# Folding the first batch's short chunk ahead of its products, in a Fourier-mixing and gated feed-forward kernel

## The chip, the cores and the metric

The kernel runs on one core of one Trainium2 chip. The metric is the device time of one execution in microseconds (us). Engine names are those of the profile: PE is TensorE's matmul, PEld its weight load, DVE is VectorE, ACT ScalarE, POOL GpSimd, SP SyncE, which here issues DMAs.

## The reference

```python
def reference(x, moe_w_gate, moe_w_val, moe_w_out):   # x: 8 x 3008 x 256
    X = np.fft.fft(x, axis=1)
    X = np.fft.fft(X, axis=2)
    a = X.real.astype(np.float32).reshape(8 * 3008, 256)
    g = a @ moe_w_gate                                  # 256 x 1536
    silu = g * (1.0 / (1.0 + np.exp(-g)))
    val = a @ moe_w_val
    return (silu * val @ moe_w_out).astype(np.float32)  # 1536 x 256
```

So there is a real part of a two-dimensional Fourier transform of each batch (over 3,008 rows and 256 columns), and then a gated feed-forward layer on each of the 24,064 rows. Inputs and output are float32.

## The kernel before

**The mathematics.** The kernel does not transform the columns (called d) of x. It folds that transform into the weights: `Wp` and `Wq` are the gate and value weights multiplied by a cosine table `CD` and a sine table `SDt` (`half_w` for the first 512 columns of the weights, `weight_op` inside the main loop for the other two blocks of 512). `Wm` is `Wq` with rows scaled by the column `m2`, for the mirrored rows of the output. What is left of the transform over rows is done by products with tables of cosines and sines (`Tab`), on data that has been folded by symmetry: row n with row M - n, and quarters with each other. The results are `Pt` (even part) and `Qt` (odd part), tiles of up to 512 transformed rows, which are the moving operand of the feed-forward products.

**Chunks.** The rows of a batch's quarter are cut into a long chunk of 128 (A) and a short one of 60 (C). For the first batch, `place` puts rows in order by a product with a 0/1 matrix (`putA`, `putC`) into PSUM; `sums` adds (k = 0) or subtracts (k = 1) the falling rows from SBUF into `SA` (chunk A) and `SC` (chunk C), on DVE; `fold_d` folds SA over d on POOL into `EOA`, which ACT copies as bfloat16 to `EOb`, and `half_folded` multiplies that by the tables. For chunk C, `direct` writes unfolded halves `SBc` on DVE straight from PSUM, and `unfolded` multiplies both halves, 16 products in all. `row0` adds the products of the column d = 0. `transform` copies one half of the result by ACT (`od`) and adds or subtracts it on DVE to write `Pt` and `Qt`. In this start-up the order on each engine is the order written in the code.

**The part for the odd rows.** The second part of the first batch (job (0, 1)) needs `BBa` for chunk A and `BBc` for chunk C, which lies in `St`. Before the change POOL makes them in the main loop's time out of EOA and SC: `quarter_rows` twice, and for each of two q a sum, a difference and five scalings by the row signs `sgn` and `sgo`.

**The main loop.** Its units (t, f) are 24 tiles t of up to 512 rows and 12 blocks f of 128 hidden columns. Each unit has gate and value products in PSUM (`g` and `v`, three buffers each), Silu on ACT, products on DVE or POOL into `hp` and `hm`; `OWork` multiplies these by `Wo` (`o`, two buffers), ACT evicts and SP stores. Which engine does what is read from `KINDS`, one digit a unit: bit 1 has the odd row added ahead by ACT ("seed", L1425), bit 2 has the gate split (two gate products of PE instead of three, with work on DVE), the higher bits give products to POOL; "w" (tile 0 and two units of tile 1) is a unit with all six products.

**The planner.** The main loop is not written in order. `S.add` collects operations with an engine, a duration that the author assumed, what they read, write and need; `S.run` then plays a list schedule over the engines and emits the instructions in that order. `SHIFT` and `BIAS` (per tile and kind of operation) move due times; `S.run` is told from when each engine is free. DMA arrivals are stand-ins with an assumed latency. The chip runs each engine's instructions in that order, each waiting for its inputs.

**Queues.** Loads of x for the first batch go out on SP and on ACT's queue, weight loads on POOL's queue, in `load_w`: W0 (first 512 columns of the gate and value weights), then the rest into the space of `XA` (`Wraw`), in blocks of 512 columns. Loads of chunk C of batches 0 and 1 (L156 and L158) follow on SP behind two copies of zeros (L564) that wait for a memset of `zeros`. At most eight DMAs of SP are under way, since each waits for the eighth before it. `Wo` (L1978) is issued on POOL behind the BBc work.

The rows that the steps touch: L378 weight loads, L426 `place`, L435 `sums`, L492 and L493 `fold_d`, L480 `half_folded`, L487 `unfolded`, L529 `direct`, L460 to L464 `half_w`, L607 `row0`, L638 and L643 `transform`, L352 and L356 angles, L359 and L362 sines and cosines, L694 row signs, L1818 to L1833 weight blocks in the loop, L1352 gate and value products, L1387 to L1411 whole units, L1614 products with Wo.

Of the kernel before, what the change touches and what calls it, by code (L numbers as in the profile page):

```python
# [12 lines left out]
F32 = mybir.dt.float32  # L13
# [18 lines left out]
def kernel(  # L32
# [8 lines left out]
    nc = tc.nc  # L41
# [71 lines left out]
    sgn = const.tile([P, 1], F32, name="sgn")  # L113
    XA = const.tile([P, 8, 2, D], F32, name="XA")
# [6 lines left out]
    Wraw = [XAw[:, i * 4 * T:(i + 1) * 4 * T].rearrange("p (n f) -> p n f", n=2) for i in range(2)]  # L121

# [110 lines left out]
    SBc = tp.tile([P, 2, 2, 2, 2, P], BF16, name="SBc")  # L233
# [13 lines left out]
    nc.vector.memset(sel, 0.0)  # L247
    xf = XC0.rearrange("p a q d -> p (a q d)")
# [18 lines left out]
    fall_c(1, 0, nc.scalar)  # L267
    fall_c(1, 1, nc.scalar)
# [18 lines left out]
    def more_iotas():  # L287
        nc.gpsimd.memset(putC, -1.0)
        for hi in range(2):
            pm = 64 * hi + NCR  # L290
            nc.gpsimd.iota(putC[:, pm - NCR:pm], pattern=[[-2 * LC, NC_], [2, LC]], base=2 * (NCR - LC) + hi, **iota)
        pts(putC, putC, scalar1=pcol, scalar2=1.0, op0=Alu.is_equal, op1=Alu.mult)
# [41 lines left out]
    nc.vector.memset(EOf[:, 1, :, P:P + 1], 0.0)  # L334
    vts(m2, pcol, scalar1=0.0, scalar2=-2.0, op0=Alu.not_equal, op1=Alu.mult)
    vts(sgn, half, scalar1=1.0 / 32, scalar2=1.0, op0=Alu.mult, op1=Alu.add)
    sgo = const.tile([P, 1], F32, name="sgo")
    vts(sgo, pc, scalar1=float(NCR), scalar2=-2.0, op0=Alu.is_equal, op1=Alu.mult)
    vts(sgo, sgo, scalar1=1.0, scalar2=sgn, op0=Alu.add, op1=Alu.mult)
    vts(wC, pc, scalar1=float(LC - 1), scalar2=-0.5, op0=Alu.is_equal, op1=Alu.mult)  # L340
    vts(wC, wC, scalar1=1.0, scalar2=None, op0=Alu.add)
# [31 lines left out]
    def load_w(fc, only=(0, 1)):  # L373
        for i, src in ((0, moe_w_gate), (1, moe_w_val)):
            if i not in only:
                continue
            dst = W0[i] if fc == 0 else Wraw[i][:, :, (fc - 1) * T:fc * T]
            nc.gpsimd.dma_start(out=dst, in_=src.rearrange("(no p) f -> p no f", p=P)[:, :, fc * T:(fc + 1) * T])  # L378
# [7 lines left out]
    turns(ti[0], kf, 0)  # L386
    turns(ti[1], kf, 1)
    nc.gpsimd.dma_start(out=XC0[NCR:64 + NCR + 1:64, 2:4, 0],
                        in_=rows_at(0, 0, [[2 * R * D, 2], [R * D, 2], [1, D]]))
    more_iotas()  # L390
# [3 lines left out]
    tp.tile([P, 1900], F32, name="pad")  # L394

    def ce_angles(ch):
        rr, ra = ce_angle[ch]
        angles(rr, kf, ch, ti[ch])
        magnitude(ra, rr)

    def ce_tables(ch):
        rr, ra = ce_angle[ch]
        sine(ch, 0, NCE, rr)
        cosine(ch, 0, NCE, ra)

    ce_angles(0)
    nc.vector.memset(Tab[:, :, :, :, NOO - 1:NOO], 0.0)
    ce_tables(0)
    ce_angles(1)
    ce_tables(1)  # L410
# [8 lines left out]


# [15 lines left out]

    def halves(SB, S, k, a=0):

        nc.scalar.copy(SB[:, k, 0, a:a + 2], S[:, k, a:a + 2, :, P:0:-1])
        nc.scalar.activation(SB[:, k, 1, a:a + 2], S[:, k, a:a + 2, :, P:D], AF.Copy, scale=(-1.0 if k else 1.0))  # L440
# [81 lines left out]
    def direct(k):  # L522
        for a in range(2):
            down = XC0[:, 2 + a, ::-1, :]
            for hf, r_ in ((0, slice(P, 0, -1)), (1, slice(P, D))):
                x_, y_ = psC[a][:, :, r_], down[:, :, r_]
                if k and hf:
                    x_, y_ = y_, x_
                vtt(SBc[:, k, hf, a], x_, y_, op=(Alu.add, Alu.subtract)[k])  # L529
# [24 lines left out]
    direct(0)  # L554
    direct(1)
    sums(SC, 0, XC0, psC)
    start_acc(1)
    X3c = XC.rearrange("p a q d -> p (a q d)")
    zeros = Af.rearrange("p a b d -> p (a b d)")[:, 0:D]
    hd = tp.tile([P, 2, 2, 1], F32, name="hd")  # L560
    ptt(hd, SA[:, 0, 0:2, :, 0:1], SA[:, 0, 2:4, :, 0:1], op=Alu.add)
    nc.gpsimd.memset(zeros, 0.0)
# [6 lines left out]
    nc.vector.memset(SDt[:, :, 0:1], 1.0)  # L569
# [93 lines left out]
    unfolded(0, SBc)  # L663
    transform(0, 0, (0,), acc)
    for a in (0, 2):
        half_folded(1, a)
    nc.gpsimd.iota(kfO, pattern=[[4, G]], base=1, **iota)
    load_w(2)
    turns(rrO[:, 0].bitcast(I32), kfO, 0)
    turns(rrO[:, 1].bitcast(I32), kfO, 1)  # L670
    for k in range(2):
        half_w(0, k, psO, "o")
    unfolded(1, SBc)
    for q in range(2):
        row0(0, q, acc[1][q])
    sums(SC, 1, XC0, psC)
# [6 lines left out]
    for q in range(2):  # L683
        quarter_rows(ptt, EOA[:, 0, :, q, :], EOA[:, 1, :, q, :], BBa[:, q])

    for q in range(2):
        S, Dd = SC[:, 0, :, q, :], SC[:, 1, :, q, :]
        E, O = EOf[:, 0, 0:2], EOf[:, 1, 0:2]
        ptt(E[:, :, 0:P], S[:, :, P:0:-1], S[:, :, P:D], op=Alu.add)
        ptt(O[:, :, 0:P], Dd[:, :, P:0:-1], Dd[:, :, P:D], op=Alu.subtract)  # L690
        for dst, src, sg in ((BBc[:, q, 0, 0], E[:, 0, 0:P], 1.0), (BBc[:, q, 0, 1], E[:, 1, 0:P], -1.0),
                             (BBc[:, q, 1], O[:, :, 0:P], None), (BBc[:, q, 1, 0, 0:1], S[:, 1, 0:1], -1.0),
                             (BBc[:, q, 1, 1, 0:1], S[:, 0, 0:1], 1.0)):
            pts(dst, src, scalar1=sgn if sg else sgo, scalar2=sg or 1.0, op0=Alu.mult, op1=Alu.mult)  # L694


# [37 lines left out]
    def rows(r0, n, step):  # L734
# [4 lines left out]
    WP_ACT = ()  # L739
    C1_AT = 10  # L740
    A1_AT = 21
    C2_AT = 38
    A1_LOAD = 8
# [26 lines left out]
        (16, 'SP'): 3.25,  # L770
        (14, 'EV'): -1.0,
        (16, 'HP'): -2.25,
        (16, 'EG'): -1.6,
        (19, 'SM'): 2.5,
        (8, 'EG'): 1.05,
        (23, 'VM'): 3.15,
        (9, 'HP'): -2.2,
        (17, 'EV'): 0.2,
        (14, 'VG'): 4,
        (3, 'SM'): -1.5,  # L780
        (18, 'HP'): -2.5,
# [17 lines left out]
        (1, 'EG'): -1.1,  # L799
        (2, 'ES'): 2.05,  # L800
        (2, 'EV'): -1.35,
        (3, 'PUT'): -4.6,
        (3, 'SP'): 3.35,
        (3, 'VM'): -0.3,
        (4, 'ROW'): -5,
        (3, 'ROW'): 1.6,
        (3, 'HP'): -0.65,
        (3, 'EG'): -0.35,
        (0, 'HM'): 2.2,
        (0, 'EG'): -2.2,  # L810
        (0, 'HP'): -1.5,
        (0, 'VAL'): -1.2,
        (0, 'SEED'): 2.0,
        (0, 'SM'): 0.9,
        (0, 'VG'): -0.75,
        (0, 'HG'): -1.25,
        (0, 'SP'): 3.6,
        (0, 'ROW'): -0.3,
        (0, 'OD'): 4.5,
        (0, 'EV'): 0.4,  # L820
        (0, 'VM'): -0.25,
        (0, 'ES'): -1.7,
        (0, 'PUT'): 0.1,
        (1, 'EV'): 4.45,
        (1, 'ES'): 3.05,
        (2, 'SP'): -1.4,
        (1, 'SEED'): 0.9,
        (1, 'HM'): 1.95,
        (2, 'SEED'): -0.4,
        (1, 'SM'): 0.2,  # L830
        (1, 'SP'): 0.9,
        (2, 'VG'): -0.9,
        (1, 'ROW'): 1.3,
        (1, 'OD'): -1.15,
        (1, 'FOLD'): -0.15,
        (1, 'HG'): 1.6,
        (1, 'VG'): 0.15,
        (1, 'PUT'): -1.25,
        (1, 'VAL'): 0.25,
        (2, 'PUT'): 0.65,  # L840
        (2, 'VAL'): -0.25,
        (2, 'OD'): 0.75,
        (2, 'HP'): -0.75,
        (2, 'VM'): -0.5,
        (2, 'FOLD'): 0.5,
        (2, 'HG'): 0.75,
        (2, 'EG'): -0.25,
        (3, 'SEED'): 1.4,
        (3, 'OD'): 0.4,
        (3, 'HG'): -1.45,  # L850
        (3, 'GM'): -1.65,
        (3, 'EV'): 1.4,
        (3, 'VAL'): -2.2,
        (3, 'HM'): 0.55,
        (3, 'ES'): -0.85,
        (3, 'VG'): 0.1,
        (3, 'FOLD'): -0.5,
        (5, 'HM'): 2.2,
        (5, 'ROW'): -1.85,
        (4, 'VG'): 0.85,  # L860
        (4, 'HP'): 5,
        (4, 'SEED'): -2.7,
        (4, 'EG'): 3.7,
        (4, 'PUT'): -0.1,
        (4, 'SP'): -0.65,
        (4, 'OD'): 1.6,
        (4, 'VM'): 2.2,
        (4, 'HG'): -0.8,
        (4, 'HM'): 1.25,
        (4, 'SM'): -0.45,  # L870
        (4, 'VAL'): -0.5,
        (4, 'ES'): -0.35,
# [1162 lines left out]
```

## Time and profile before

| what | us |
|---|---|
| median of 3 runs (604.97 to 605.37) | 605.32 |
| the profiled execution | 605.64 |
| its span | 603.9 |
| busy PE / DVE / ACT / POOL | 595.8 / 575.9 / 564.2 / 510.2 |
| first gate product of tile 0 (L1352) starts | 21.19 |
| first product with Wo (L1614) starts | 48.52 |

The granted TensorE clock is 1.00 in every stretch of this profile. Busy time of PE is modelled from starts and lengths, so it covers small gaps. Times in the text are from the start of the span; "from ... to" of a group in the timeline runs from the first start to the last end.

### The profile page before, as it was taken

To read this page: it belongs to the slowest core of one execution; us is meant where nothing else is said; L and a number is where in the kernel's file an instruction comes from. 1 tells how busy PE (TensorE), PEld (TensorE's weight loads), DVE (VectorE), ACT (ScalarE), POOL (GpSimd) and SP (SyncE) were. 2 spreads that over 40 slices of the span, in tenths; PEclk is the share of its full clock that TensorE was granted. 3 is DMA by queue.
4 is the path that set the end of the run, shared out by engine and by line. 5 is a ranking of instruction groups with operands and counts; after the bars stand their busy time and mean duration, and the time that the engine had idled before them with its cause. 6 is when DMAs were issued, how large, how long until landed. Compare 5 with 4: busy or idle time off the path is not lost.

```text
span 603.9 us, 12610 instructions
## 1 busy us (share of the span) xinstructions
PE 595.8 (99%) x4058; PEld 392.6 (65%) x4058; DVE 575.9 (95%) x1069; ACT 564.2 (93%) x1086; POOL 510.2 (84%) x469
## 2 busy tenths in 40 slices
PE   8999999999999999999999999999999999999997
PEld 6546666666666666666666666666666666666686
DVE  9999999999999999999999999999999999999993
ACT  7798999999999999989999999999999999999994
POOL 8937999999798999996999988797997467687772
PEclk9999999999999999999999999999999999999999
DMA  8886446244715413454254112036111212111112
GB/s 228 112 148 160 112 121 176 63 129 112 198 42 123 126 60 121 120 134 115 64 115 123 53 47 81 17 102 187 50 60 38 63 46 63 37 54 51 54 53 80
DMA packets 51054, 57.91 MB, mean 96 GB/s; under 512 B 7254, under 2 KB 38170, under 8 KB 50988
## 3 DMA queue, kind: packets, MB, share of 16 engines
q1 hardware_dynamic: 47334, 53.97, 32.7%
q0 software_dynamic: 3216, 2.36, 3.2%
q10 hardware_dynamic: 438, 0.77, 0.5%
q8 instruction: 32, 0.52, 0.4%
q14 instruction: 34, 0.28, 0.2%
HBM read 29.43 MB, written 24.65 MB: 90 GB/s over the span
## 4 chain that ended last, share of the span: by engine, by line
PE 86%; ACT 3%; POOL 3%; DMA 2%; issue 1%; DVE 1%; SPq 0%; ACTq 0%; POOLq 0%
PE o L1614 38%; PE g L1352 25%; PE v L1352 18%; PE g L1770 2%; PE o L1770 2%; DMA XA<-in_x_dram 1%; POOL hm L1563 1%; PE v L1614 1%; POOL SDf L174 1%; ACT sg L1408 0%; ACT sg L1387 0%; DMA out_dram<-ev 0%; PE o L601 0%; PE g L601 0%; PE o L1818 0%
## 5 line engine op out<-in xcount | busy, mean ns | idle before, releaser
L1563 POOL TENSOR_TENSOR hm<-sv 128x1024 bf16<-128x1024 f32 (+2 forms) x137 | 254.6, 1862 | 55.5 <-ACT sv L1539 21.2
L1555 DVE SCALAR_TENSOR_TENSOR sv<-es,v 128x512 f32<-128x512 f32 (+2 forms) x266 | 176.8, 671 | 6.2 <-PE v L1352 3.3
L1566 DVE TENSOR_TENSOR hp<-sp,v 128x512 bf16<-128x512 f32 (+2 forms) x241 | 160.6, 672 | 4.6 <-PE v L1352 2.3
L1614 PE MATMUL o<-Wo,hm 128*128 128x256 bf16 (+1 forms) x1128 | 162.5, 273 | 0.0
L1614 PE MATMUL o<-Wo,hp 128*128 128x256 bf16 (+1 forms) x1104 | 159.8, 272 | 0.0
L1614 PEld LDWEIGHTS <-hm 128*128 128x128 bf16 (+2 forms) x1140 | 111.8, 98 | 56.5 <-issue 1.7
L1614 PEld LDWEIGHTS <-hp 128*128 128x128 bf16 (+2 forms) x1140 | 111.9, 98 | 55.4 <-issue 1.5
L1539 ACT ACTIVATE sv<-g 128x512 f32<-128x512 f32 (+2 forms) x181 | 117.9, 673 | 4.3 <-PE g L1352 2.2
L1464 ACT ACTIVATE sp<-g 128x512 f32<-128x512 f32 (+2 forms) x181 | 111.6, 625 | 3.1 <-PE g L1352 2.1
L1425 ACT ACTIVATE v<-bc,w 128x512 f32<-128x512 bf16 (+2 forms) x151 | 107.9, 718 | 3.0 <-DVE hm L1411 1.2
L1352 PE MATMUL g<-Pt,Wp 128*128 128x512 bf16 (+2 forms) x288 | 107.9, 375 | 0.2 <-DVE Qt L643 0.2
L1352 PE MATMUL v<-Pt,Wp 128*128 128x512 bf16 (+2 forms) x288 | 105.2, 374 | 0.7 <-ACT v L1425 0.6
L1352 PE MATMUL g<-Qt,Wq 128*128 128x512 bf16 (+2 forms) x288 | 105.1, 375 | 0.0
L1487 ACT ACTIVATE es<-v 128x512 f32<-128x512 f32 (+2 forms) x151 | 93.3, 620 | 2.5 <-DVE sv L1555 1.1
L1489 DVE SCALAR_TENSOR_TENSOR es<-bc,w,v 128x512 f32<-128x512 bf16 (+2 forms) x123 | 90.1, 735 | 2.6 <-PE v L1352 1.1
L1352 PEld LDWEIGHTS <-Wp 128*128 128x128 bf16 x576 | 56.2, 98 | 27.4 <-issue 1.6
L1352 PE MATMUL g<-Qt,Wm 128*128 128x512 bf16 (+2 forms) x195 | 72.9, 376 | 0.5 <-ACT sg L1387 0.3
L1468 DVE SCALAR_TENSOR_TENSOR sg<-bc,w,g 128x512 f32<-128x512 bf16 (+2 forms) x93 | 67.2, 724 | 1.6 <-PE g L1352 1.3
L1539 ACT ACTIVATE sv<-sg 128x512 f32<-128x512 f32 (+2 forms) x93 | 64.5, 698 | 0.9 <-DVE sg L1532 0.9
L1532 DVE SCALAR_TENSOR_TENSOR sg<-sg,g 128x512 f32<-128x512 f32 (+2 forms) x93 | 61.6, 662 | 0.9 <-PE g L1352 0.4
L1352 PE MATMUL v<-Qt,Wm 128*128 128x512 bf16 (+2 forms) x165 | 61.6, 374 | 0.4 <-ACT es L1487 0.4
L1536 ACT ACTIVATE sp<-g 128x512 f32<-128x512 f32 (+2 forms) x93 | 56.9, 612 | 4.6 <-DVE sg L1532 4.4
(199 smaller groups left out, 754.3 us busy)
## 6 DMA issues: line engine op xcount, KB each, us to landing
out_dram<-ev SPq DMA_DIRECT2D x96, 128.0 KB
XA<-in_x_dram SPq DMA_DIRECT2D x30, 256.0 KB
XA<-in_x_dram SPq DMA_DIRECT2D x112, 64.0 KB
XC<-in_x_dram SPq DMA_DIRECT2D x30, 120.0 KB
XC<-in_x_dram SPq DMA_DIRECT2D x105, 32.0 KB
bc<-br SPq DMA_DIRECT2D x19, 128.0 KB
St<-Fc SPq DMA_DIRECT2D x12, 128.5 KB
out_dram<-ev SPq DMA_DIRECT2D x12, 120.0 KB
```

The costliest lines, as they stand in the source:

```text
L1352: nc.tensor.matmul(ps[:, :n], Wt[:, gv, fs], src[:, :n], start=start, stop=stop, skip_group_check=True)
L1425: nc.scalar.activation(T_[kv][:, :w], bc[t][:, :w], AF.Copy, scale=w0[:, 1, f:f + 1])
L1464: nc.scalar.activation(sp_to()[:, :w], T_[kg][:, :w], AF.Silu)
L1468: nc.vector.scalar_tensor_tensor(T_[keg][:, :w], bc[t][:, :w], w0[:, 0, f:f + 1], T_[kg][:, :w], op0=Alu.mult, op1=Alu.add)
L1487: nc.scalar.activation(T_[kes][:, :w], T_[kv][:, :w], AF.Copy, scale=2.0 if on_pool(u) > 1 else 1.0)
L1489: nc.vector.scalar_tensor_tensor(T_[kes][:, :w], bc[t][:, :w], w0[:, 1, f:f + 1], T_[kv][:, :w], op0=Alu.mult, op1=Alu.add)
L1532: nc.vector.scalar_tensor_tensor(T_[kgm][:, :w], T_[keg][:, :w], 2.0, T_[kg][:, :w], op0=Alu.mult, op1=Alu.subtract)
L1539: nc.scalar.activation(sv()[:, f % 2, w - 1::-1, 1], T_[kgm if by_dve else kg][:, :w], AF.Silu)
L1555: nc.vector.scalar_tensor_tensor(sv()[:, f % 2, w - 1::-1, 0], T_[kes][:, :w], 2.0, T_[kv][:, :w], op0=Alu.mult, op1=Alu.subtract)
L1563: nc.gpsimd.tensor_tensor(hts_(t)[1][:, f - 1:f + 1, :w], sv()[:, :, :w, 1], sv()[:, :, :w, 0], op=Alu.mult)
L1566: nc.vector.tensor_tensor(hts_(t)[0][:, f, :wp], T_[ksp][:, :wp], T_[kv][:, :wp], op=Alu.mult)
L1614: nc.tensor.matmul(st["ps"][:n, j, :], hts[t][minus][:, f, c:c + n], Wo[:, f, :], start=(f == 0), stop=(f == nF - 1))
```

## The change

It has four parts.

1. Chunk C of the first batch is folded over d by DVE (`fold_c`, from SC into a bfloat16 tile `EB` that lies in EOf) before its products: `folded_c` issues 8 products where `unfolded` issued 16. `direct` and `SBc` go. ACT later scales EB by row signs into BBc (`signed_op`, at unit 8); two one-column products on DVE write BBc's column 0. POOL's loop over q goes, and its two `quarter_rows` become three operations over both q.
2. The sums of chunk A are ordered by pairs of quarters (sum and difference of a pair together), both accumulators are begun early, `half_folded(1, 0)` stands before `place(XC0)`, and 8 + 4 warm products on PE stand where there were 28.
3. The rest of the weights comes in two DMAs of 1,024 columns instead of four of 512. Two x loads move from ACT's queue to SP's. The memsets of `zeros` and `Z0` move from POOL to the opening of DVE, the row signs and weights from DVE to POOL, the d tables ahead of the sines on ACT.
4. The planner's inputs change: `WM_ACT` is empty (all four Wm blocks on POOL), `WP_ACT` gives one Wp block to ACT, `KINDS` of tiles 1 to 16, `BIAS` of tiles 0 to 17, unit numbers of folds, the assumed arrival of weights and the times from which engines are free. From tile 18 on KINDS and BIAS are the same.

```diff
+    nc.vector.memset(Z0, 0.0)
+    zeros = Af.rearrange("p a b d -> p (a b d)")[:, 0:D]
...
-    fall_c(1, 0, nc.scalar)
-    fall_c(1, 1, nc.scalar)
+    fall_c(1, 0, q)
+    fall_c(1, 1, q)
...
+    vts(rrd, prod, scalar1=D - 1, scalar2=None, op0=Alu.bitwise_and)
+    def row_weights():
+        pts(wC, pc, scalar1=float(LC - 1), scalar2=-0.5, op0=Alu.is_equal, op1=Alu.mult)
+        pts(wC, wC, scalar1=1.0, scalar2=1.0, op0=Alu.mult, op1=Alu.add)
+        pts(putC, putC, scalar1=pcol, scalar2=1.0, op0=Alu.is_equal, op1=Alu.mult)
+    def row_signs():
+        pts(m2, pcol, scalar1=0.0, scalar2=-2.0, op0=Alu.is_gt, op1=Alu.mult)
+        pts(sgn, half, scalar1=1.0 / 32, scalar2=1.0, op0=Alu.mult, op1=Alu.add)
+        pts(nsgn, sgn, scalar1=-1.0, scalar2=1.0, op0=Alu.mult, op1=Alu.mult)
...
-    def load_w(fc, only=(0, 1)):
+    def load_w(first, only=(0, 1)):
...
-            dst = W0[i] if fc == 0 else Wraw[i][:, :, (fc - 1) * T:fc * T]
-            nc.gpsimd.dma_start(out=dst, in_=src.rearrange("(no p) f -> p no f", p=P)[:, :, fc * T:(fc + 1) * T])
+            if first:
+                nc.gpsimd.dma_start(out=W0[i], in_=w_[:, :, 0:T])
+            else:
+                nc.gpsimd.dma_start(out=Wraw[i][:, :, 0:Dff - T], in_=w_[:, :, T:Dff])
...
+    d_tables()
+    sine(0, 0, NCE, ce_angle[0][0])
...
-    def unfolded(eo, SB):
+    def folded_c(eo):
         for a in range(2):
             for q in range(2):
                 dst, rhs = set_cols(acc[eo][q], Tab[:, 1, q, eo], a)
-                for hf in range(2):
-                    nc.tensor.matmul(dst, SB[:, eo, hf, a, q, :], rhs, start=False, stop=(a == 1 and hf == 1),
-                                     skip_group_check=True)
+                nc.tensor.matmul(dst, EB[:, eo, a, q, :], rhs, start=False, stop=a == 1, skip_group_check=True)
+    def fold_c(eo):
+        s_ = SC[:, eo]
+        vtt(EB[:, eo], s_[:, :, :, P:0:-1], s_[:, :, :, P:D], op=(Alu.add, Alu.subtract)[eo])
...
     psA = place(XA, putA, 4, ((psG, "g"), (psV, "v")))
-    warm(28)
-    sums(SA, 0, XA, psA, (0, 1))
-    vts(rrd, prod, scalar1=D - 1, scalar2=None, op0=Alu.bitwise_and)
-    sums(SA, 0, XA, psA, (2, 3))
-    opposite(0)
+    warm(8)
+    for a0 in (0, 2):
+        sums(SA, 0, XA, psA, (a0, a0 + 1))
+        sums(SA, 1, XA, psA, (a0, a0 + 1))
+    start_acc(0)
+    start_acc(1)
     fold_d(0, 0)
+    load_w(1, (0,))
     weigh_ce()
-    load_w(0, (0,))
+    half_folded(0, 0)
+    warm(4)
+    fold_d(1, 0)
+    load_w(1, (1,))
+    half_folded(1, 0)
+    psC = place(XC0, putC, 2, ((psG, "g"), (psV, "v")))
+    opposite(1)
     fold_d(0, 2)
-    load_w(0, (1,))
-    opposite(1)
-    d_tables()
-    sums(SA, 1, XA, psA)
-    start_acc(0)
-    half_folded(0, 0)
-    if 0:
-        warm(0)
-    psC = place(XC0, putC, 2, ((psG, "g"), (psV, "v")))
+    fold_d(1, 2)
+    load_w(0)
     half_folded(0, 2)
-    for a in (0, 2):
-        fold_d(1, a)
-    load_w(1)
-    direct(0)
-    direct(1)
-    sums(SC, 0, XC0, psC)
-    start_acc(1)
+    half_folded(1, 2)
+    for k, a in ((0, 0), (1, 0), (0, 1)):
+        sums(SC, k, XC0, psC, (a,))
+    fold_c(0)
+    nc.vector.memset(SDt[:, :, 0:1], 1.0)
+    sums(SC, 1, XC0, psC, (1,))
+    fold_c(1)
+    for k in range(2):
+        vts(BBc[:, :, 1, k, 0:1], SC[:, 0, 1 - k, :, 0:1], scalar1=(nsgn, sgn)[k], scalar2=None, op0=Alu.mult)
...
-    WP_ACT = ()
+    WP_ACT = ((1, 1),)
...
-    WM_ACT = ((1, 0), (1, 1))
+    WM_ACT = ()
+    SIGN_AT = 8
...
+    def signed_op():
+        for k, sg in enumerate((sgn, nsgn)):
+            S.add("ACT", 0.3, lambda k=k, sg=sg: nc.scalar.activation(BBc[:, :, 0, k], EB[:, 0, k], AF.Copy, scale=sg),
+                  r=[(("fold",), "E")], w=[(("st", 0), k)])
+        S.add("ACT", 0.5, lambda: nc.scalar.activation(
+            BBc[:, :, 1, :, 1:P], EB[:, 1, :, :, 1:P].rearrange("p a q d -> p q a d"), AF.Copy, scale=sgo),
+              r=[(("fold",), "E")], w=[(("st", 0), 0)])
...
-    for fc, at in ((1, 0.0), (2, 4.0)):
+    for fc in (1, 2):
         for gv in range(2):
-            S.add("DMA", 0.01, lambda: None, w=[(("W",), (fc, gv))], lat=at + gv)
+            S.add("DMA", 0.01, lambda: None, w=[(("W",), (fc, gv))], lat=1.5 * gv)
...
-    S.run({'DVE': 1.2, 'ACT': 0.7, 'POOL': 13.0, 'PE': 0.0})
+    S.run({'DVE': 1.2, 'ACT': 0.9, 'POOL': 3.0, 'PE': 0.0})
```

In the changed program the products of weight blocks stand at L1804 (L1818 before) and the loop's gate and value products at L1338 (L1352 before).

More of the change, by code (lines that the diff above doesn't have):

```diff
@@ L662 @@
     first_tile = {(b, part): tile_of(b * H + part * 2 * G) for b, part in jobs}
-    unfolded(0, SBc)
+    folded_c(0)
     transform(0, 0, (0,), acc)
[L665 to L670, printed above, removed]
     for k in range(2):
         half_w(0, k, psO, "o")
-    unfolded(1, SBc)
+    folded_c(1)
     for q in range(2):
         row0(0, q, acc[1][q])
-    sums(SC, 1, XC0, psC)
     transform(0, 0, (1,), acc)
@@ L682 @@
         nc.scalar.activation(Wm[:, :, fs], Wq[:, :, fs], AF.Copy, scale=m2)
[L683 to L694, printed above, removed]
+    nc.gpsimd.iota(kfO, pattern=[[4, G]], base=1, **iota)
+    turns(rrO[:, 0].bitcast(I32), kfO, 0)
+    turns(rrO[:, 1].bitcast(I32), kfO, 1)
+    E_, O_ = EOA[:, 0].rearrange("p a q d -> p q a d"), EOA[:, 1].rearrange("p a q d -> p q a d")
+    ptt(BBa[:, :, 0], E_[:, :, 0:4:3, 0:P], E_[:, :, 2:0:-1, 0:P], op=Alu.subtract)
+    ptt(BBa[:, :, 1], O_[:, :, 0:2, 0:P], O_[:, :, 2:4, 0:P], op=Alu.subtract)
+    ptt(BBa[:, :, 1, :, 0:1], E_[:, :, 3::-3, P:P + 1], E_[:, :, 1:3, P:P + 1], op=Alu.subtract)
     tmp_ctx.close()
@@ L817 @@
[L817 to L836, printed above, removed]
@@ new lines @@
+        (6, 'PUT'): -2.6,
+        (6, 'ROW'): -1.1,
+        (6, 'VG'): 0.9,
+        (6, 'HM'): 0.6,
+        (6, 'OD'): -1.5,
+        (7, 'HP'): 0.25,
+        (6, 'ES'): -0.5,
+        (7, 'ROW'): -0.95,
+        (7, 'GM'): -2.25,
+        (7, 'HM'): 0.15,
+        (7, 'SM'): 0.5,
+        (7, 'OD'): -1,
+        (7, 'HG'): 0.25,
+        (7, 'VG'): 1,
+        (7, 'VM'): -0.5,
+        (7, 'SP'): 0.25,
+        (8, 'ES'): 1.4,
+        (8, 'SM'): -0.85,
+        (8, 'OD'): -0.3,
+        (8, 'VAL'): 1.85,
@@ L1699, in fn @@
                 if kind == "A":
-                    queue[what] = fold_steps(nc.gpsimd, XA, *coef_a(b), q, slice(0, P))
+                    queue[what, q] = fold_steps(nc.gpsimd, XA, *coef_a(b), q, slice(0, P))
                 else:
@@ L1907 @@
               17: [lambda: S.add("POOL", 0.8, halve_tables, w=[(("Tab",), "z")])],
-              6: [lambda: S.add("POOL", 0.5, clear_d0, w=[(("Z0",), k) for k in range(2)])]}
+              6: []}
+    before.setdefault(SIGN_AT, []).append(signed_op)
     def row_width(t):
```

596 lines of the change are left out of this document (288 added, 308 removed).

## The prediction

> **What bounds the kernel now.** I read the busy totals first, then busy time by stretch, then the start-up in the timeline, then the DMA issues. The busy totals:
>
> ```profile
> PE 595.8 (99%) x4058; PEld 392.6 (65%) x4058; DVE 575.9 (95%) x1069; ACT 564.2 (93%) x1086; POOL 510.2 (84%) x469
> ```
>
> PE is the bound, but its busy time is modelled, so I count its work instead. From the first gate product (21.19 us) on, the kernel issues 3,910 matmuls: 1,198 of 512 columns, 2,280 of 256, 130 of 480, 278 between 188 and 377 and 24 of one column. In the chain of waits eight of 256 columns take 0.87 us (0.109 each) and four of 512 take 0.86 (0.215 each), so a matmul costs 0.417 ns a column plus 2.5 ns (25 ns each for the one-column ones). That is 571.1 us of dense work. The last matmul ends at 599.8, so PE stood still for about 7.5 us after 21.19. By start-to-start gaps 2.7 us of that lie before 48.5, 4.3 us between 48.5 and 430, the rest later, where the order of the changed program is nearly or wholly the old one. Busy time by stretch (columns: stretch, length, PE, PEld, DVE, ACT, POOL, clock, DMA share, GB/s):
>
> ```profile
> 21.19:48.50 27.31, 26.04 (x146) 12.17 (x144) 25.98 (x51) 25.90 (x48) 14.79 (x26) 1.00 0.78 125
> 48.50:200.00 151.50, 150.31 (x1024) 100.14 (x1023) 145.44 (x258) 142.84 (x275) 145.35 (x137) 1.00 0.47 128
> ```
>
> In the first stretch DVE and ACT are as full as PE: there the eviction engines pace PE. So three things count: when the first gate product starts, how much DVE and ACT hold PE up in tile 0, and the gaps of the middle. The start-up, in order of time:
>
> ```profile
> 9.59 1.09 POOL L492 TENSOR_TENSOR EOA<-SA 128x512 f32<-128x512 f32 x1 [1.21 <-DVE SA L435]
> 10.62 0.82 POOL L378 DMA_DIRECT2D W<-in_moe_w_gate_dram  x1
> 12.04 1.10 PE L426 MATMUL g<-XC,putC 128*128 128x512 f32 x2
> 12.59 0.62 ACT L493 CAST EOb<-EOA 128x512 bf16<-128x512 f32 x1 [0.44 <-POOL EOA L492]
> 13.55 0.76 DVE L529 TENSOR_TENSOR SBc<-g,XC 128x256 bf16<-128x256 f32 x2
> 16.20 0.68 DVE L435 TENSOR_TENSOR SC<-g,XC 128x512 f32<-128x512 f32 x1
> 20.59 1.27 DVE L643 TENSOR_TENSOR Qt<-g,od 128x188 bf16<-128x188 f32 x6
> 17.28 1.48 SPq L564 DMA_DIRECT2D XC<-Af  x2
> 18.80 12.20 SPq L156 DMA_DIRECT2D XC<-in_x_dram  x15
> ```
>
> DVE works without a break from 8.29 to 22.4; the last columns of Qt and the second Wp copy release tile 0. The DMA issues (KB, us to landing):
>
> ```profile
> XA<-in_moe_w_gate_dram POOLq DMA_DIRECT2D x2, 256.0 KB, 6.6
> XA<-in_moe_w_val_dram POOLq DMA_DIRECT2D x2, 256.0 KB, 8.2
> W<-in_moe_w_gate_dram POOLq DMA_DIRECT2D x1, 256.0 KB, 4.6
> W<-in_moe_w_val_dram POOLq DMA_DIRECT2D x1, 256.0 KB, 5.0
> ```
>
> **The change, part by part.** *Opening, to the first sum.* DVE loses seven one-column operations (3.88 to 4.62, 0.7 us) and gains the Z0 memset (64 words took it 0.11, 256 took POOL 0.33, so 0.3 to 0.7 for 384; I take 0.35), the zeros (0.3) and rrd (0.25, moved from between the sums). The ScalarE queue loses two DMA issues (3.20 to 5.54), so prodd comes near 3.1 instead of 5.6 and the d tables (four rows, 1.5 us) go ahead of the sines at no cost: ACT stood idle there. Their issues go to SP, which stood idle from 3.33 to 6.0 and has room for the 2.3 us; past that, rise_c would come later by the rest. The sums begin near 8.4 instead of 8.29. POOL gains seven one-column operations (0.20 to 0.27 each, L694 and L444) ahead of its first fold, which moves from 9.59 to about 9.8; who reads them (weigh_ce, place C, the two one-column products) comes 1.5 us later or more.
>
> *Sums, folds, place C.* The eight SA sums follow each 0.60 apart as before and end near 13.3. But place(XC0) now stands on PE behind half_folded(1, 0), which waits for a second POOL fold behind a weight DMA: 9.8, fold 1.09, issue 0.82, fold 1.10, cast 0.62, four products at 0.16, with 0.05 a hand-over, gives 14.1. Its first pair takes 1.1 (12.04 to 13.14), so SC can start near 15.3, and DVE stands idle for 2 us. That is the price of the new order.
>
> *From SC to the first gate product.* Gone: eight direct operations (13.55 to 16.28, 2.7 us) and sixteen products of 377 columns; new: two folds of 512 columns, two one-column operations, eight products. No row shows a DVE fold with both inputs in SBUF: the 512-column sums take 0.68, POOL's fold 1.10, the 377-column rr operation 0.60 to 0.85; I take 0.7 of the range 0.6 to 1.1, as the sums are nearest. Three SC sums 15.3 to 17.15, first fold to 17.85, products 0.64 and the od copy 0.47 to 19.0; meanwhile fourth sum, second fold and two small ones keep DVE until 19.3. Six Pt puts 1.2, Wp copy 0.68: 21.2. The second od is there at 21.1 (eight half_w products 0.87, four products 0.64, row0 0.65, copy 0.47), so Qt runs 21.2 to 22.4. The second pair of half_w needs the PSUM tile that the Wp copy frees at 21.2; eight products later, at 22.1, the first gate product starts, against 21.19: **+0.9** (0.4 to 1.6).
>
> *PE's work in the main loop.* The listing has one 512-column product more (one gate split fewer): **+0.2**. The 16 warm products and eight others that go lie in waiting time: nothing. Half the weight issues (two of 0.73) go on POOL; that is cover for its own turns, not path.
>
> *Tile 0.* DVE loses one Wp copy (0.68). ACT loses two Wm copies (0.70 each), gains a Wp copy (0.59) and three sign operations (0.5 each by the 512-column copies, halved for 256; 1.1 together). POOL loses the BBc work (25.9 to 33.2, 7.3 us); two Wm more (0.69 each) fit there. The Wo load, issued at 33.19 and 11.8 us on its way, goes out near 25, and the listing puts the first Wo product after 18.4 us of matmuls instead of 24.1: PE has work that needs neither DVE nor ACT. ACT's queue from its first sg (24.0) to its first od is 18 sg at 0.455, four Wq at 0.50, four sines at 0.83 and 2.0 for the rest, 15.5 us, for 15.5 us of matmuls that began 1.9 us sooner and may run some 0.7 ahead; later ACT catches up. So PE loses some 1.3 us before it reaches the place of 48.5, where it lost 2.7: **-1.4** (-2.2 to 0).
>
> *The middle.* The listing has five seeds fewer (ACT 0.72 + 0.62 each off, 0.735 each onto DVE) and three products more on POOL with their copies (0.6 on ACT): ACT -4.9 us, DVE about -1. With the gaps at 4.3 us and their releasers DVE and ACT, I take **-0.9**; the new order could as well cost 2 or save 2.5.
>
> Sum: 0.9 + 0.2 - 1.4 - 0.9 = -1.2. The profiled execution took 605.64 (span 603.9 and 1.7 around it), 0.3 above the median, so 604.4 there and 604.1 against the median. About 0.2% (1.2 us) is what a measurement of this kernel tells from no change; the forecast sits at that edge.
>
> **Rivals.** *Late weights (slower).* The zeros now come from DVE near 8.4, so SP's two L564 issues and the XC loads, held until 17.28 and 18.80 by POOL's memset, follow near 9.8 and share the DMA engines with W0 and the weight rest. W0 landed in 4.6 to 5.0 us without them, the rest in 6.6 to 8.2 beside them. PE needs the whole val rest after 4.1 us of products, at 26.4; issued at 16.6 it lands at 24.8 if 8.2 holds. But four pieces took from 15.3 to about 28.8 (19.1 + 9.7, the longest landing); if the rest takes that long again, it lands near 29, PE waits 2.9 and some 0.6 comes out of later gaps: 606.5 to 607. It decides from a landing past 26.4. The Trainium skill, DMA: Bandwidth & Descriptors, "Why a DMA increments its semaphore by 16 and not by 1", says that a copy uses the largest number of DMA engines up to 16 that divides both slowest dimensions, so a four-partition XC load would burden four engines and a weight load would wait for those; by it this rival holds. The trace, which names no engine, agrees in that the last weight landed at 9.7 us beside such loads.
>
> *A colder clock (slower).* 28 warm products become 12, and by my chain PE idles 1.2 us before each half_folded. The granted clock is 1.00 in every stretch, but the first 52 products took 4.62 us where the 28 took 1.73. If PE ran at half rate from 11 on, the products on the path (first pair of folds 0.6, place C 1.1, folded_c and half_w 1.2 each time) would double and cost some 2.9: 607.0. The Trainium skill, TensorE: Matmul & The Clock Gate, "What's actually happening", gives an idle window of about 3.4 us before half rate; by that no gap here is long enough.
>
> *The order does not fit (slower).* The planner sees the weights at 0 and 1.5 us and POOL free at 3.0; if the middle gains 2 us of gaps instead of losing 0.9: 607.0.
>
> *More gain.* Middle gaps shrink by 2.2 and tile 0 by 1.6: 602.7. Nothing goes lower, as the dense work stays. That fewer DMAs mean fewer bytes isn't so: 1,024 KB either way.
>
> **Chances.** Forecast 0.48 (own range 603.1 to 605.5; 0.31 faster, 0.17 same); late weights 0.22 (0.18 slower, 0.04 same); clock 0.06 slower; order 0.10 (0.08 slower, 0.02 same); more gain 0.14 faster. Faster 0.45, same 0.23, slower 0.32. The range 602.7 to 607.0 leaves out the ends of the rivals.
>
> **What would show it.** Right: DVE idle about 2 us ahead of SC near 15.3; first gate product near 22.1; no PE wait for a DMA at L1804; fewer than 1.5 us of gaps in tile 0; Wo landed before 40. Wrong: SC before 14.5, a first gate product before 21.2 or past 23, a weight product released by a DMA, a clock under 1.00, or middle gaps above 5 us.

## The result, and the profile after

The changed kernel is slower: 610.72 us (median of 4 runs, 610.21 to 612.68) against 605.35 for the kernel before (4 runs, 604.97 to 605.67), a ratio of 1.0095 with a 95% interval of 1.0072 to 1.0118. Its profiled execution took 610.45, with a span of 608.6. The forecast was 604.1, with a range of 602.7 to 607.0.

First the page's busy totals and its row of the granted clock (40 equal slices, in tenths of full speed):

```profile
PE 592.9 (97%) x3978; PEld 391.9 (64%) x4035; DVE 573.7 (94%) x1058; ACT 559.9 (92%) x1081; POOL 510.3 (84%) x462
...
PEclk9899999999999999999999999999999999999999
```

No engine has more work than before (POOL 0.1 us), and yet the span is 4.7 us longer. The second slice (15 to 30 us) has a clock of 8 where the others have 9. So the loss is in the start-up, and its timeline comes next (start, length, engine, line, operation; in brackets the idle time ahead of it and what ended it):

```profile
10.01 1.48 SPq L565 DMA_DIRECT2D XC<-Af  x2
11.54 16.68 SPq L160 DMA_DIRECT2D XC<-in_x_dram  x15
...
13.10 0.74 POOL L388 DMA_DIRECT2D W<-in_moe_w_val_dram  x1
...
15.73 1.29 DVE L447 TENSOR_TENSOR SC<-g,XC 128x512 f32<-128x512 f32 x2 [2.32 <-PE g L438]
18.91 0.69 DVE L447 TENSOR_TENSOR SC<-v,XC 128x512 f32<-128x512 f32 x1 [1.89 <-issue]
...
20.39 0.34 PE L493 MATMUL v<-Tab,EOf 128*128 128x377 bf16 x1 [2.70 <-DVE SDt L556]
...
22.96 0.58 PE L467 MATMUL o<-W,CD 128*128 128x256 bf16 x2 [1.54 <-DMA W<-in_moe_w_val_dram]
...
28.24 0.38 PE L1338 MATMUL g<-Pt,Wp 128*128 128x480 bf16 x1 [0.50 <-DVE Qt L643]
```

SP sends the two copies of zeros at 10.01 and the fifteen chunk C loads of batch 1 from 11.54 on, 7.3 us sooner than before. The third sum of SC waits 1.89 us; the label says "issue", but the wait was on the count of the last XC0 load and ended 0.04 us after that load's last piece landed (18.83). Then PE waits for the value half of W0 (L467), and the first gate product starts at 28.24 instead of 21.19. The clock by stretch, with the same columns as before, and the DMA issues:

```profile
22.00:24.00 2.00, 1.04 (x6) 0.71 (x6) 1.84 (x9) 0.00 (x0) 2.00 (x5) 0.74 0.95 186
24.00:26.00 2.00, 2.00 (x9) 0.92 (x8) 0.27 (x1) 0.58 (x1) 2.00 (x2) 0.50 0.43 93
```

```profile
XA<-in_moe_w_gate_dram POOLq DMA_DIRECT2D x1, 512.0 KB, 10.2
XA<-in_moe_w_val_dram POOLq DMA_DIRECT2D x1, 512.0 KB, 13.2
W<-in_moe_w_gate_dram POOLq DMA_DIRECT2D x1, 256.0 KB, 9.2
W<-in_moe_w_val_dram POOLq DMA_DIRECT2D x1, 256.0 KB, 9.8
```

The two halves of W0 took 9.2 and 9.8 us to land, where they took 4.6 and 5.0: that is the fault in two rows. From 22.95 to 26.36 PE ran at half rate. From the first gate product to the end of the last matmul it took 576.8 us, 1.8 less than before (578.6). So 7.05 us were lost ahead of it and 1.8 won behind it.

### The profile page after: what moved, and what is told of

Same layout as the page of the kernel before. It is cut to its first block, busy times and chain, and to the rows that moved or that the text cites. A ratio compares the mean times of both kernels' runs of the same rounds, so it can differ in the third digit from the quotient of the medians.

```text
span 608.6 us, 12502 instructions
## 1 busy us (share of the span) xinstructions
PE 592.9 (97%) x3978; PEld 391.9 (64%) x4035; DVE 573.7 (94%) x1058; ACT 559.9 (92%) x1081; POOL 510.3 (84%) x462
## 4 chain that ended last, share of the span: by engine, by line
PE 83%; DVE 4%; issue 2%; POOL 2%; ACT 2%; DMA 1%; SPq 0%; DVEq 0%; ACTq 0%
PE o L1600 36%; PE g L1338 23%; PE v L1338 18%; PE g L1756 2%; PE o L1756 2%; DVE sv L1541 1%; DVE hp L1552 1%; POOL hm L1549 1%; DVE es L1475 1%; PE v L1600 1%; DMA XC<-in_x_dram 0%; POOL SDf L178 0%; DVE sg L1518 0%; ACT sp L1450 0%; PE g L601 0%
## 5 line engine op out<-in xcount | busy, mean ns | idle before, releaser
L1552 DVE TENSOR_TENSOR hp<-sp,v 128x512 bf16<-128x512 f32 (+2 forms) x238 | 157.7, 670 | 5.2 <-PE v L1338 4.0
L1525 ACT ACTIVATE sv<-g 128x512 f32<-128x512 f32 (+2 forms) x182 | 120.9, 679 | 3.8 <-PE g L1338 3.3
L1411 ACT ACTIVATE v<-bc,w 128x512 f32<-128x512 bf16 (+2 forms) x146 | 105.4, 723 | 2.1 <-DVE sv L1541 1.0
L1338 PE MATMUL g<-Pt,Wp 128*128 128x512 bf16 (+2 forms) x280 | 104.7, 375 | 1.5 <-ACT sp L1522 0.7
L1338 PE MATMUL v<-Pt,Wp 128*128 128x512 bf16 (+2 forms) x287 | 105.6, 375 | 0.4
L1475 DVE SCALAR_TENSOR_TENSOR es<-bc,w,v 128x512 f32<-128x512 bf16 (+2 forms) x128 | 93.1, 732 | 3.2 <-PE g L1338 0.5
L1473 ACT ACTIVATE es<-v 128x512 f32<-128x512 f32 (+2 forms) x146 | 90.4, 621 | 4.6 <-PE v L1338 2.5
L1338 PE MATMUL g<-Qt,Wq 128*128 128x512 bf16 (+2 forms) x250 | 91.9, 374 | 0.4
L1338 PEld LDWEIGHTS <-Wp 128*128 128x128 bf16 x576 | 56.1, 97 | 26.3 <-DVE Qt L643 0.8
L1338 PE MATMUL g<-Qt,Wm 128*128 128x512 bf16 (+2 forms) x192 | 71.9, 376 | 0.5
L1338 PEld LDWEIGHTS <-Wq 128*128 128x128 bf16 x430 | 41.9, 98 | 27.6 <-issue 3.5
```

The source lines that it names most:

```text
L1338: nc.tensor.matmul(ps[:, :n], Wt[:, gv, fs], src[:, :n], start=start, stop=stop, skip_group_check=True)
L1411: nc.scalar.activation(T_[kv][:, :w], bc[t][:, :w], AF.Copy, scale=w0[:, 1, f:f + 1])
L1473: nc.scalar.activation(T_[kes][:, :w], T_[kv][:, :w], AF.Copy, scale=2.0 if on_pool(u) > 1 else 1.0)
L1475: nc.vector.scalar_tensor_tensor(T_[kes][:, :w], bc[t][:, :w], w0[:, 1, f:f + 1], T_[kv][:, :w], op0=Alu.mult, op1=Alu.add)
L1525: nc.scalar.activation(sv()[:, f % 2, w - 1::-1, 1], T_[kgm if by_dve else kg][:, :w], AF.Silu)
L1552: nc.vector.tensor_tensor(hts_(t)[0][:, f, :wp], T_[ksp][:, :wp], T_[kv][:, :wp], op=Alu.mult)
```

## The experiments

My theory was that the early zeros alone cause the loss: DVE's memset lets SP's queue run 7 us sooner, into the weight loads. The rivals were the clock (12 warm products for 28), the order of `place(XC0)`, and the planner. Each median below stands with its ratio to the kernel before on the same chip. The table gathers what the traces show (us). A DMA reports its landing in sixteen pieces; the landings here are those of the last piece, by the landing events of the trace. The columns before the median are of one execution each: of 605.21 us with the zeros late (next to the lowest of eleven), of 609.08 with the loads held (the highest of five), and in the other kernels within 0.9 us of the median.

| kernel | XC0 landed | W0 value landed | half rate after 15 us | first gate product | median | ratio (interval) |
|---|---|---|---|---|---|---|
| before | 13.8 | 17.5 | 0 | 21.19 | 605.35 | |
| changed | 18.8 | 22.9 | 3.41 | 28.24 | 610.72 | 1.0095 (1.0072 to 1.0118) |
| zeros late | 13.8 | 17.7 | 0 | 23.12 | 606.10 | 1.0010 (1.0001 to 1.0019) |
| before, zeros early | 14.2 | 22.1 | 6.83 | 28.43 | 612.05 | 1.0103 (1.0088 to 1.0118) |
| changed, PE filled | 14.2 | 22.6 | 0 | 27.55 | 610.11 | 1.0077 (1.0063 to 1.0091) |
| changed, loads held | 15.4 | 21.0 | 3.41 | 26.27 | 607.30 | 1.0031 (1.0018 to 1.0044) |
| changed, one load | 14.5 | 26.1 | 6.83 | 31.42 | 614.17 | 1.0145 (1.0131 to 1.0158) |
| one load, rest held | 13.9 | 23.5 | 3.41 | 28.78 | 611.52 | 1.0105 (1.0091 to 1.0119) |

**Zeros late.** The changed kernel with the one memset put back:

```diff
-    nc.vector.memset(zeros, 0.0)
...
     ptt(hd, SA[:, 0, 0:2, :, 0:1], SA[:, 0, 2:4, :, 0:1], op=Alu.add)
+    nc.gpsimd.memset(zeros, 0.0)
```

> The changed kernel with one step put back: the zeros are written by POOL behind the first one-column sum of its heads again, as before the change, so SP's two copies of zeros and the fifteen loads of chunk C of batch 1 go out near 17.5 us instead of 10.0. Theory (early loads: what runs on SP from 10.0 holds up the last piece of XC0 to 19.1 and the first value weights to 22.9, and the half clock from 22.9 to 26.4 is only its sequel): the last XC0 load lands near 13, the value weights before 18, no stretch at half clock, the first gate product starts at 21.5 to 23.0 instead of 28.2, and the time is 604 to 605.5. Rival (clock: 12 warm products instead of 28 let PE cool): half rate stays somewhere before 30 us and the time is 608 or more. Rival (place of XC0 behind a second fold on POOL): the first gate product is not before 25, the time 607 or more.

Its timeline and DMA issues:

```profile
17.92 1.48 SPq L565 DMA_DIRECT2D XC<-Af  x2
...
15.59 1.29 DVE L446 TENSOR_TENSOR SC<-g,XC 128x512 f32<-128x512 f32 x2 [2.44 <-PE g L437]
...
18.92 0.60 PE L466 MATMUL o<-W,CD 128*128 128x256 bf16 x4
...
23.12 0.38 PE L1338 MATMUL g<-Pt,Wp 128*128 128x480 bf16 x1
```

```profile
W<-in_moe_w_gate_dram POOLq DMA_DIRECT2D x1, 256.0 KB, 4.1
W<-in_moe_w_val_dram POOLq DMA_DIRECT2D x1, 256.0 KB, 4.6
```

The weights land in 4.1 and 4.6 us again, `half_w` (L466) runs without a wait for a DMA, the clock of this execution stays at 1.00 with the same 12 warm products, and 5.1 of the 7.05 us are back. The median, 606.10, is 0.6 above what I expected at most, and the trace does not show why: in its execution (605.21) the last matmul ended at 599.82, as in the kernel before (599.81), so that the rest of the change just paid for its later start (23.12 against 21.19). In three of the other executions (606.55 to 606.87) the granted clock averaged 0.997, as in the changed kernel's profile. Half rate may have come there too, but no trace shows it.

**Zeros early in the kernel before.** The same step alone:

```diff
+    zeros = Af.rearrange("p a b d -> p (a b d)")[:, 0:D]
     nc.vector.memset(Tab[:, :, :, :, NOO - 1:NOO], 0.0)
+    nc.vector.memset(zeros, 0.0)
...
-    nc.gpsimd.memset(zeros, 0.0)
```

> The kernel before with that one step alone: the zeros are written by DVE in the opening, so the copies and the chunk C loads go out near 10 us. Nothing else is changed (28 warm products, old order, old weights, old planner). Theory (early loads): the first value weights land 4 to 6 us later than 17.5, the first gate product starts 3 to 6 us later than 21.2, and the time is 607 to 611. Rivals (clock, place, planner): within 0.5 us of 605.35.

```profile
19.75 0.38 PE L462 MATMUL o<-W,CD 128*128 128x256 bf16 x2 [2.21 <-DMA W<-in_moe_w_gate_dram]
22.15 0.59 PE L462 MATMUL o<-W,CD 128*128 128x256 bf16 x2 [2.02 <-DMA W<-in_moe_w_val_dram]
...
28.43 0.37 PE L1352 MATMUL g<-Pt,Wp 128*128 128x480 bf16 x1
```

In the timeline PE waits for both halves of W0. The kernel before loses 6.7 us by this one step, with its 28 warm products, its order and its planner untouched (1 us more than expected at most; here 6.83 us ran at half rate, whose price no run tells apart in this kernel). So the step is enough by itself, in either kernel.

**PE filled.** It asks what the clock costs (the new argument of `half_w` puts 30 warm products between its gate and its value products):

```diff
     half_folded(1, 2)
+    warm(50)
...
-        half_w(0, k, psO, "o")
+        half_w(0, k, psO, "o", 0 if k else 30)
```

> The changed kernel with early zeros kept, and PE kept busy where it stood idle: 50 warm products ahead of folded_c(0) and 30 between the gate and the value products of the first half_w. Theory (early loads): the clock stays at 1.00, but the last XC0 load and the value weights land as late; only the products that ran at half rate come faster, at most 1.7 us: first gate product 26.5 to 28, time 609.0 to 610.5. Rival (clock): the first gate product comes back to 22 to 24, time 604 to 606.

```profile
17.53 2.95 PE L459 MATMUL o<-sel 128*128 128x128 bf16 x50
...
21.18 1.84 PE L459 MATMUL o<-sel 128*128 128x128 bf16 x30
22.86 0.38 PE L469 MATMUL o<-W,CD 128*128 128x256 bf16 x2
...
27.55 0.38 PE L1341 MATMUL g<-Pt,Wp 128*128 128x480 bf16 x1 [0.56 <-DVE Qt L646]
```

The timeline shows PE covered up to 23 us, and the clock was 1.00 throughout; the first gate product came 0.7 us sooner and no more. From the first product that reads the value half to the first gate product it took 4.69 us here (from 22.86) and 5.28 in the changed kernel (from 22.96). So the half rate is a sequel that cost about 0.6 us. One part of my theory fell: here XC0 landed at 14.2 and SC did not wait, and the start was nearly as late. This run alone says little of that, as its 50 warm products hold the chunk C products back until 20.32. But in "before, zeros early" and in "one load, rest held" below, which have no such products, XC0 landed at 14.2 and 13.9, and the start was as late. So XC0's late landing, which I had seen only in the changed kernel's profile, is not needed. The value half of W0 is: in the five runs with early zeros in the changed kernel the first gate product follows its landing by 5.0 to 5.3 us. The distance alone proves nothing (it is 5.4 with the zeros late, where no product waited for a DMA); the waits for the value half in the timelines do.

**Loads held.** Which of the early transfers hurt? One word on POOL into rows that the first chunk C load writes keeps the loads back, and the copies of zeros stay early:

```diff
     ptt(hd, SA[:, 0, 0:2, :, 0:1], SA[:, 0, 2:4, :, 0:1], op=Alu.add)
+    nc.gpsimd.memset(XC[64:68, 0:1, 0, 0:1], 0.0)
```

> The changed kernel with early zeros kept; a one-word memset on POOL (behind the first one-column sum of the heads) into rows that the first chunk C load of batch 1 writes holds that load, and those behind it on SP, to about 17.7 us. The two copies of zeros still go at 10.0. It tells the copies from the loads. If the loads are what hurts: as with the zeros late, 605.5 to 607. If the copies of zeros are: the last XC0 load still lands past 17, time 608.5 to 611.

```profile
9.92 1.49 SPq L566 DMA_DIRECT2D XC<-Af  x2
17.85 12.72 SPq L160 DMA_DIRECT2D XC<-in_x_dram  x15
...
19.76 0.39 PE L467 MATMUL o<-W,CD 128*128 128x256 bf16 x2 [0.66 <-DMA W<-in_moe_w_gate_dram]
21.02 0.38 PE L467 MATMUL o<-W,CD 128*128 128x256 bf16 x2 [0.87 <-DMA W<-in_moe_w_val_dram]
```

The median, 607.30, lies 0.3 above the expected band: loads and copies both hurt. How the loss is shared is not settled. Between the changed kernel and "zeros late" the loads account for 3.4 of 4.6 us by the medians, for 2.0 of 5.1 by the first gate product, and for 1.4 of 5.2 by the profiled executions (610.45, 609.08 and 605.21). The landing events show what the copies do. Of the sixteen pieces of W0's gate half twelve landed at 16.19 to 17.71 and the other four at 19.23 to 19.71; of its value half twelve at 18.77 to 19.34 and four at 20.41 to 20.98. With the zeros late all sixteen landed at 14.97 to 15.26 and at 17.07 to 17.72. The twelve pieces of the gate half were late by 1.2 us and more before any of the held loads went out (17.85), so that is not the loads' doing; in the lateness of the last four the loads may have a share.

**One load for fifteen.** Is it the four-partition form of the loads?

```diff
+        if b == 1:
+            ups = [lambda: q.dma_start(out=X3[p0:p0 + NCR, 0:4, :], in_=up_block(b, JC - LC * (NC_ - 1), NCR))]
+            ups += [lambda: None] * (NC_ - 1)
```

> The changed kernel with early zeros kept; only the fifteen loads of four partitions each (chunk C of batch 1) are one load of 60 partitions with the same bytes, the rows in another order of blocks, so the values of batch 1 are not the reference's. It tells apart why the early loads hold up the others. If it is their form (the four pieces of each go to a few DMA engines and the last pieces of other transfers wait there): the last XC0 load and the first value weights land within 1.5 us of where they did with the zeros late (13.8 and 17.7), the first gate product starts at 23 to 24.5, time 605.5 to 607.5. If it is the bytes (480 KB more ahead of the weights): the value weights land past 20, time 608.5 to 611.

It came out outside both bands, at 614.17. The reason is that the edit did two things: with one DMA in place of fifteen the limit of eight under way no longer held back the four loads behind it, and those went out from 13.15 on. So the run could not tell form from bytes, and I repeated it with those loads held by a word on POOL as above:

> As with the one load of 60 partitions (zeros early, batch 1's values not the reference's), and the loads behind it on SP held to about 17.7 by a one-word memset on POOL, so that only the 480 KB of the one load, and no more than the fifteen carry, go out early. The copies of zeros go at 10.0 as before. Form (fifteen loads of four partitions are what hurts beyond the copies): near the run with the loads held, 606.8 to 608.3, value weights landing by 21.5. Bytes (480 KB ahead of the weights cost the same in any form): 609 to 612, value weights landing past 22.5.

```profile
11.17 1.97 SPq L163 DMA_DIRECT2D XC<-in_x_dram  x1
...
23.50 0.59 PE L471 MATMUL o<-W,CD 128*128 128x256 bf16 x2 [2.78 <-DMA W<-in_moe_w_val_dram]
```

611.52, with the value half landing at 23.46: by the bands that I had set, the case of the bytes. So the four-partition form is not what it takes; one load of 60 partitions costs as much. That the cost goes by the bytes is not shown, as the bytes ahead of the weights were not the same: when the value half landed in the changed kernel (22.92), nine of the fifteen loads had been issued (288 KB), while the one load sent all 480 KB at 11.17. The form changes which pieces wait. With fifteen four-partition loads, twelve pieces of the value half landed by 19.57 and four at 21.64 to 22.92; with one load, twelve by 22.20 and four at 23.31 to 23.46. The Trainium skill, DMA: Bandwidth & Descriptors, "Why a DMA increments its semaphore by 16 and not by 1", has a copy run on the largest number of engines up to 16 that divides both slowest dimensions, so a four-partition load takes four. The split into twelve and four agrees; my conclusion from it, that spreading the load would free the weights, does not, by 611.52 against 610.72.

**What the rest of the change is worth.** On top of "zeros late", first `place(XC0)` moved one step up:

```diff
-    half_folded(1, 0)
     psC = place(XC0, putC, 2, ((psG, "g"), (psV, "v")))
+    half_folded(1, 0)
```

> As the first of these (zeros late), and place of XC0 one step up in PE's order, ahead of half_folded(1, 0) instead of behind it. It weighs the price that the forecast put on the new order (DVE idle 2 us before SC). If that wait is on the path: SC starts 1 to 1.5 us sooner, the first gate product 0.7 to 1.5 us sooner than with the zeros late alone, and the time is 0.5 to 1.5 us lower. If not (the fold of the second pair on POOL or the weights set the start): within 0.4 us of it.

604.96 (ratio 0.9994, interval 0.9985 to 1.0002): SC starts at 14.16 instead of 15.59, the first gate product at 21.98 instead of 23.12, and the time falls by 1.1 us by the medians (in the profiled executions the last matmul ends 0.54 sooner). DVE's wait ahead of SC was on the path to the first gate product. Then the row signs out of POOL's way:

```diff
     row_weights()
-    row_signs()
...
     nc.gpsimd.tensor_copy(EOA[:, 0, :, :, P:P + 1], SA[:, 0, :, :, 0:1])
+    row_signs()
```

> Zeros late and place one step up, and in addition the five one-column row-sign operations of POOL (8.74 to 10.2) moved from ahead of its first fold to behind the column copy of EOA, with the two one-column products that need them (DVE, 18.0 to 18.7) behind the last half_w. If the folds of POOL set the start: first fold near 9.6 instead of 10.17, everything to the first gate product 0.4 to 0.7 sooner (21.3 to 21.6 instead of 21.98), time 604.2 to 604.7. If the sums of DVE and place set it: the first gate product stays at 21.7 to 22.0 and the time within 0.3 us of 604.96.

The first gate product came at 21.42, as expected, but the time is 604.80 (0.9992, 0.9984 to 1.0001): by the ratios 0.1 us less, not 0.3 to 0.7. The 0.56 us of earlier start went into tile 0: PE's idle time there rose from 1.41 to 1.68, and by 0.2 behind it, so that the last matmul ended 0.08 sooner (599.20). The timeline shows where PE stands first:

```profile
22.29 2.48 DVE L361 SCALAR_TENSOR_TENSOR XA<-XA,mM 128x376 f32<-128x376 f32 x2
24.68 1.21 DVE L1376 TENSOR_TENSOR hp<-sg,v 128x480 bf16<-128x480 f32 x2
...
25.38 0.36 PE L1338 MATMUL v<-Qt,Wm 128*128 128x480 bf16 x1 [0.69 <-DVE hp L1376]
```

Two odd angles stand on DVE ahead of the first evictions. I tried to move them:

```diff
-    before = {2: [lambda: weight_op(1, 0), lambda: angle_op(0)], 3: [lambda: weight_op(1, 1), lambda: cosine_op(0)],
+    before = {2: [lambda: weight_op(1, 0)], 3: [lambda: weight_op(1, 1), lambda: angle_op(0), lambda: cosine_op(0)],
```

> The version with the signs later, and the first two odd angles (DVE L361, 22.3 to 24.8, where the second took 1.62 us beside POOL's BBa) asked for one unit later, behind the first evictions of tile 0. If they are what keeps PE waiting 0.7 us at 24.6: the idle time of tile 0 falls by 0.5 to 0.8 and the time to 604.0 to 604.4. If the planner's order in later tiles, which shifts with it, gives that back: 604.6 to 606, with larger gaps past 100 us.

605.79 (1.0007, 0.9998 to 1.0016), within the second band; but the edit did not do what it was for. The two angles stayed at 22.26, since DVE's order there came out the same, and the order of later tiles changed: the last matmul ended at 600.28 instead of 599.20, with the first gate product at the same 21.41. What the two angles cost stays open. Last, the old planner inputs on top of "zeros late" and the earlier `place`:

```diff
-    WP_ACT = ((1, 1),)
+    WP_ACT = ()
...
-        "06ww21000310",
+        "02ww25021100",
```

(C1_AT to A1_LOAD, BIAS, WM_ACT and the rest of KINDS likewise.)

> Zeros late and place one step up, with the old planner inputs in the changed kernel: KINDS, BIAS, unit numbers, WM_ACT (two Wm blocks on ACT) and WP_ACT (none) as before the change; the new signed operations stay. By the forecast the new inputs save 0.9 us in the middle (48.5 to 430) and part of the 1.4 in tile 0, so the time is 1 to 2 us above 604.96, the idle time of PE from 48 to 430 some 0.9 larger. Rival (the inputs only move gaps about): within 0.5 us of 604.96. Rival (old inputs don't fit the new start): over 607.

607.24 (1.0029, 1.0018 to 1.0041), 2.3 above the version with the new inputs (2.1 by the ratios): the second rival's case. PE's idle time is 0.6 larger in tile 0 (2.00 against 1.41) and 2.1 larger from there up to 401.8 us of work (5.78 against 3.65). So the new inputs fit the new operations; the old ones do not.

## Why the prediction was wrong, step by step

PE's idle time is counted as in the prediction, from start to start against dense work, cut at the same amounts of work (24.6 and 401.8 us, where the kernel before reaches 48.5 and 430). The prediction's 4.3 us for the middle added up the positive gaps alone; with the steps between products that came out shorter than their dense work it is 3.81. For the changed program I use "zeros late", which has the same order but for the memset and lacks no matmul records (the changed kernel's trace lacks 57).

| step | forecast | measured |
|---|---|---|
| first gate product, zeros late | +0.9 | +1.9 |
| the same, zeros early as changed | (rival: not moved) | +7.05 |
| PE work | +0.2 | +0.2 |
| idle time of tile 0 | -1.4 | -1.9 (2.70 to 0.76) |
| idle time of the middle | -0.9 | -0.1 (3.81 to 3.68) |
| idle time after | 0 | -0.1 |

**The step that failed** is "from SC to the first gate product". It let `half_w` wait for a PSUM tile only and took W0 as landed. The late-weights rival did see that SP's queue would run early, but it kept W0's 4.6 and 5.0 us and looked for the damage at the val rest, needed at 26.4 (L1804), for 606.5 to 607. Right mechanism, wrong transfer. W0 goes out on POOL at 11.2 and 13.1, right behind the early loads; it is needed some 8 us sooner than the rest, and nothing hides it. The rows for the price were there. In the kernel before, the two 256 KB blocks of weights that went out beside these same chunk C loads (at 18.39 and 19.11) took 8.6 and 9.7 us, the two ahead of them (15.32 and 16.05) 4.6 and 6.7; the listed 6.6 and 8.2 are the middles of such pairs. 9.7 from 13.1 gives 22.8, where the value half landed at 22.92. That is some 4 us past the place where the forecast's chain has `half_w`, and with its 0.9 makes some 5 us of start. So late weights should have been the forecast. (In that rival's own sum 22.1 and 4.1 make 26.2, not 26.4, which changes nothing.)

**The size of the start-up without the early loads** was off by 1.0. SC began at 15.59 (15.3 forecast). The fourth sum, second fold and two one-column operations took from 18.14 to 20.13, 2.0 us where I had 1.45: the fold waits for the end of the sum that it reads, and the first one-column operation took 0.56. The Qt puts ended at 23.07 (22.4 forecast), and the first gate product followed at 23.12. The forecast had let it start at 22.1, ahead of its own end of the Qt puts; in the changed order it waits for them (in the changed kernel's timeline 0.50 us on DVE's Qt, L643).

**Tile 0 and the middle.** Tile 0 gained more than forecast and within its range. Wo went out at 26.49 and landed 12.0 us later, before 40 as said. The middle gained 0.1 of the 0.9, an allowance that rested on ACT's smaller load; the gaps there did not follow that load. Together the main loop is 1.9 us shorter with zeros late, against 2.1 forecast.

**The rivals.** The colder clock came, with 3.41 us at half rate, but as a sequel of the waits: the filled run puts it at about 0.6 us. The order does not fit: refuted, the middle did not gain 2 us of gaps but lost 0.1, and the old inputs are the ones that do not fit (+2.3). More gain: its tile 0 came, its middle did not, and the start ate it.

**The signs.** Of the right ones, DVE's idle time ahead of SC (2.32 us), tile 0 below 1.5 and Wo's landing held. No product at L1804 waited for a DMA, but L467 did: the sign was tied to the wrong line. Of the wrong ones, a first gate product past 23, a weight product released by a DMA and a clock under 1.00 all appeared.

With the zeros late alone the changed kernel is 0.1% slower than before by the medians (1.0001 to 1.0019). With the two moves of order as well it stands at 604.80 against 605.54 (0.9984 to 1.0001): no difference that the measurement can tell. So apart from the zeros the change as made gains nothing, and with the two moves at most about 0.2%.

## What to carry to other kernels

Moving a memset can move a whole DMA queue: when an operation releases transfers, list every transfer behind it on that queue, and then every load that is under way at the new time, by when it is needed. The first to suffer is the load that is needed soonest, not the largest one. And a start-up that ends sooner is worth less than it shows when the next stage has its own pace (here 1.14 us of start gave 0.54 at the last matmul, and 0.56 more gave 0.08).

## What the runs showed of the hardware

- With the loads held, two 64 KB copies of zeros over four partitions went out at 9.92 and 10.73, just ahead of the 256 KB gate half (11.23). Twelve of its sixteen pieces landed at 16.19 to 17.71, four at 19.23 to 19.71; without the copies all sixteen landed at 14.97 to 15.26.
- Half rate came in stretches of 3.41 us or twice that, in five traces, each time 17.07 us (five times 3.41) after the first record of full rate; in the other traces full rate lasted 175 to 177 times 3.41 us. So the clock seems to change at steps of 3.41 us only, and where a wait of PE falls on these steps would matter; that is inferred. In the step ahead PE had been busy 0.4 us in three of the five. But in the changed kernel it had been busy 1.0 of the 3.41 us, with no gap above 2.70, and with the loads held 1.5 of 3.41, with no gap above 0.87; a step with 1.57 (changed kernel, 16.12 to 19.53) did not bring half rate. The Trainium skill, TensorE: Matmul & The Clock Gate, "What's actually happening", gives an idle window of about 3.4 us before half rate. The length agrees; that the window must be idle does not, by these two runs, and the measurement decides. In the prediction I had read it as a wholly idle stretch.
- A DVE operation of 376 columns with two inputs in SBUF (L361) took 0.60 us in the changed kernel, where POOL ran nothing beside it, and 1.62 in "signs later", where POOL's BBa operations (512 columns, inputs in SBUF too) ran beside it throughout. The BBa operation took 1.56 us there and 1.27 in the changed kernel, with no such operation beside it.
